# A small second transform on quarters of TensorE, with its neighbours' banks and small passes rearranged

## The chip, the cores and the metric

One core of one Trainium2 chip. The metric is the time of one execution in device microseconds (us). Engines: PE is TensorE (matrix products), DVE VectorE, ACT ScalarE, POOL GpSimd, SP the engine that issues nearly all DMAs here.

## What is computed

The reference runs three layers, one behind the other, in fp32:

```python
# x: (8, 3072, 256)
X = np.fft.rfft(x, axis=1)
Yr = Xr @ w_r - Xi @ w_i + b_r
Yi = Xr @ w_i + Xi @ w_r + b_i
# soft threshold of Yr and Yi at 0.01
y = np.fft.irfft(Yr + 1j * Yi, n=3072, axis=1)      # -> 24576 tokens x 256
logits = y @ phi                                     # 32 slots
d = exp(logits - logits.max(0)); d /= d.sum(0)       # over all tokens
slot_out = experts(d.T @ y)                          # relu(s @ w1[e]) @ w2[e]
c = softmax(logits, axis=1)
z = c @ slot_out
h = z @ w_in;  solu = h * softmax(h);  out = layernorm(solu) * g_ln @ w_out
```

## The kernel before

The program has two phases. Phase 1 (`phase1`, some 600 us) does everything up to the slots' sums; phase 2, which the change leaves alone, does the experts and the last layer over 192 blocks of 128 tokens.

Phase 1 takes the 8 batches b one after the other. A batch's transform over 3072 positions is split: 3072 = 96 x 32. The **first transform** (`stage1`, line 242, or `stage1_first` for batch 0, line 232) works along the 96, in eight units u of a batch; its products, here `s` in the trace (PSUM tile `s1`, two banks), use four quarters of the PE array of 64 rows by 64 columns. ACT copies them to SBUF (`asb`), and SP stores them to a DRAM tensor `ad` (`a_fold`, `a_out`), from which `load_ap` reads `apt` in another order. The **second transform** (`stage2`, line 273) turns `apt` with the constants `d2_sb` into the spectrum `xps` (PSUM, one bank): four products per tile t, each of 128 rows by 128 columns. Half of the entries of `d2_sb` are zero, since the even and the odd frequencies each need 64 of the 128 rows. A batch has 12 such tiles t.

Of `xps` ACT makes a copy of the imaginary part (`xi`, line 291) and the rounded copy `xh` (line 292), DVE the sum `xsum` (line 293) and the rest `xl` (line 294). For t = 0 DVE also makes `xd` and its two parts, and zeros one column of `xh` and `xl` (lines 295 to 303, `zero4`). `stage2s` rounds the sum: `sh` on ACT, `sl` on POOL (line 309). `mix` (line 313) multiplies with the weights into `pb` and `pa`; DVE adds (`yb`, lines 337 and 341) and clips (line 349), POOL subtracts (`s`, line 350). `st_transpose` (line 355) turns `s` on PE into the PSUM tile `sps`, a bank of its own from the pool `pst`, and ACT copies it to `st` (line 369). The bank count of phase 1 is `ps1` 2, `psx` 1, `psy` 2 (`pb`, `pa`), `pst` 1, `psm` 2: eight, all there are.

From `st` a chain of **small products** computes logits, slot softmax and slot sums of the batch: `qt`, `qtr`, `e2`, `inv1`, `ltr`, `maxt`, `maxb`, `fwd1`, `dtr`, `fwd2`, `slots`, `sums`. Each writes a PSUM tile from `pm()`, a ring of two banks (`psm`): a new tile takes the bank of the one before the last, so its first product waits until that one has been read. In the trace they go by what they read: `qt_sb`, `q_sb`, `r_sb`, `lt_sb` (their copies are `lg_sb`), `mx`, `d_sb`, `dt_sb` (copies: `dm_sb`), `dm_sb,w_sb`, and `s,dh_sb` for the slots, whose result DVE adds to `acc` (line 777). A running maximum over the batches (`mrun`, `rescale`, `rexp`) gives two factors `mexp`; with them DVE rescales `acc` (line 756) and `srun` (line 814).

The order of the work is a list: one loop over the 96 tiles calls the large steps, and `tick()` (four times in each round) runs what `after(lag, ...)` has put on a heap for that tick; the lags stand in the table `LAG`. Every engine runs its own instructions strictly in this order. One round, called a step here and named by the t that `mix` takes, is on PE:

```python
s1_next(need); tick(); stage2(t + 1); tick()
st_transpose(t - 2); tick()
stage2s(t + 1); mix(t); tick()
```

that is: a small product or none, `s` (in 8 of 12 steps), `xps` of the next tile, small products, the transposes of `s` of two tiles before, small products, `pb`, `pa`.

Of the kernel before, what the change touches and what calls it, by code (L numbers as in the profile page):

```python
# [35 lines left out]
def kernel(  # L36
# [109 lines left out]
    def phase1(pl: ExitStack, pr_: ExitStack):  # L146
# [84 lines left out]

        def stage1_first(ch):
            if ch == 0:
                ad[0] = dram2.tile([32, 4, 24, D], F32, name="ad", tag="ad")
            dst = s_p.tile([96, 2, D], F32, name="a0", tag="s")
            after(LAG["a_out"], a_out, 0, 2 * ch, 2, dst)
            pool, tag = ((ps1, "s1"), (pst, "sps"), (psm, "pm"))[ch % 3]
# [17 lines left out]
        def a_fold(b, n, t):  # L255
            for c in range(2):
                SP.dma_start(out=ad[b][n:n + 4, 2 * c:2 * c + 2].rearrange("n k g d -> (k g) n d"), in_=t[64 * c:64 * c + 48])

        def a_out(b, n, k, t):
            SP.dma_start(out=ad[b][n:n + k].rearrange("n k g d -> (k g) n d"), in_=t)  # L260
# [366 lines left out]

        def dsub(b, z):
            sl = slice(16 * z, 16 * z + 16)
            lg = small["lg", b].rearrange("p a (l s) -> p (a l) s", l=4)[:, sl]  # L630
            m = small["mb", b].rearrange("p (o s) -> p o s", o=1).to_broadcast([96, 16, 32])
            DVE.tensor_tensor(out=small["d", b][:, sl], in0=lg, in1=m, op=ALU.subtract)
# [947 lines left out]
```

## Time and profile before

| | |
|---|---|
| time, median of 3 runs | 1306.96 us (1306.07 to 1310.65) |
| profiled execution, its own time | 1307.97 us |
| its span, first to last instruction | 1306.2 us |
| phase 1, until the experts' first product | some 598 us |
| PE busy | 1263.1 us (97%) |
| DVE / ACT / POOL busy | 1127.9 / 988.0 / 1010.7 us |
| mean granted clock of TensorE | 0.993 |

The profile is of one execution. Busy time of PE counts products in flight, so a high share alone doesn't tell that PE is at its peak; the chain of work that ended last, the busy time of single stretches, and the instructions in order of time do. Instructions that run into each other on an engine (ACT starts one about 0.1 us before the one ahead of it ends) are each listed with their full length.

### The profile page before, as it was taken

The page shows a single profiled execution, that of the slowest core. Times are in us where ns is not written, and L with a number is a line of the kernel's source. Part 1 is how long each engine was busy: PE and PEld are TensorE (multiplying, and loading weights), DVE is VectorE, ACT ScalarE, POOL GpSimd, SP SyncE. Part 2 cuts the span into 40 slices and gives each one's busy share as a digit, 9 for nine tenths or more (in the row PEclk, how much of TensorE's full clock was granted, in tenths as well). Part 3 has the DMA queues.
Part 4 walks back from the last instruction along what each step waited for, and adds up shares of the span by engine and source line. Part 5 has one row for each costly group of instructions (what it writes and reads, how often), then busy time and mean ns, then how long its engine had stood idle before and what let it go on. Part 6 is the DMA issues. An engine that isn't in the chain of part 4 may idle for free.

```text
span 1306.2 us, 30976 instructions
## 1 busy us (share of the span) xinstructions
PE 1263.1 (97%) x11042; PEld 1115.7 (85%) x11042; DVE 1127.9 (86%) x1568; ACT 988.0 (76%) x1831; POOL 1010.7 (77%) x1114
## 2 busy tenths in 40 slices
PE   6989999999999999899699999999999999999998
PEld 2867878787878878865699999999999999999998
DVE  1867887888788888765999999999999999999995
ACT  3545556565656565543799999999999999999996
POOL 0868686877778775433589999999999999998995
PEclk8999999999999999999999999999999999999999
DMA  8986465564747364259467777777777787777874
GB/s 269 279 229 191 125 176 165 142 198 122 203 118 223 100 200 144 93 186 351 99 168 203 194 192 208 178 196 195 187 203 180 185 229 191 187 198 178 211 180 127
DMA packets 181338, 241.79 MB, mean 185 GB/s; under 512 B 21984, under 2 KB 137056, under 8 KB 181184
## 3 DMA queue, kind: packets, MB, share of 16 engines
q1 hardware_dynamic: 180736, 238.62, 67.2%
q8 instruction: 88, 1.44, 0.5%
q10 hardware_dynamic: 448, 1.18, 0.3%
q14 instruction: 66, 0.54, 0.1%
HBM read 92.00 MB, written 59.11 MB: 116 GB/s over the span
## 4 chain that ended last, share of the span: by engine, by line
PE 82%; DVE 7%; DMA 3%; issue 2%; POOL 2%; ACT 2%; SPq 1%; DVEq 0%; ACTq 0%; POOLq 0%
PE po L89 37%; PE pb L89 9%; PE pm L89 8%; PE xps L89 7%; PE hps L89 6%; PE s L89 5%; PE pa L89 4%; PE sps L92 2%; DVE st L1167 2%; DVE u L1182 2%; PE hps L92 2%; DMA xc<-in_x_dram 1%; PE pm L92 1%; DMA t<-tb 1%; DVE tb L1205 1%
## 5 line engine op out<-in xcount | busy, mean ns | idle before, releaser
L1277 POOL TENSOR_TENSOR ul<-t,uh 128x512 fp32r<-128x512 f32 x336 | 431.2, 1301 | 43.4 <-ACT uh L1263 42.6
L89 PEld LDWEIGHTS po<-gw,uh 128*128 128x128 f32 x2736 | 347.3, 188 | 14.0
L89 PE MATMUL po<-gw,uh 128*128 128x256 f32 x2736 | 353.6, 280 | 0.0
L1167 DVE TENSOR_REDUCE st<-hps 128x1 f32<-128x1024 f32 x192 | 229.1, 1194 | 10.3 <-PE hps L89 10.3
L1182 DVE SCALAR_TENSOR_TENSOR u<-hps,e 128x1024 f32<-128x1024 f32 x192 | 232.1, 1209 | 0.5 <-ACT e L1174 0.3
L1174 ACT ACTIVATE e<-hps,st 128x1024 f32<-128x1024 f32 x192 | 215.4, 1122 | 16.8 <-DVE st L1167 16.8
L89 PE MATMUL po<-gw,ul 128*128 128x256 f32 x1620 | 228.1, 284 | 0.0
L1287 ACT ACTIVATE sq<-u,st 128x1024 f32<-128x1024 f32 x192 | 223.0, 1161 | 0.3 <-DVE u L1182 0.3
L1205 DVE STREAM_TRANSPOSE tb<-u 128x1024 f32<-128x1024 f32 x169 | 210.5, 1246 | 5.9
L89 PEld LDWEIGHTS po<-gw,ul 128*128 128x128 f32 x1620 | 206.1, 188 | 1.1
L350 POOL TENSOR_TENSOR s<-yb,s 128x512 f32<-128x512 f32 x95 | 124.4, 1310 | 103.9 <-DVE s L349 99.9
L1263 ACT ACTIVATE uh<-t 128x768 fp32r<-128x768 f32 x169 | 143.4, 849 | 0.0
L89 PEld LDWEIGHTS xps<-d_sb,apt 128*128 128x128 f32 x768 | 95.0, 194 | 54.7 <-issue 28.5
L89 PE MATMUL xps<-d_sb,apt 128*128 128x128 f32 x768 | 111.3, 288 | 11.8 <-DMA apt<-ad 7.8
L252 ACT ACTIVATE asb<-s 128x1024 f32<-128x1024 f32 x56 | 57.6, 1028 | 79.9 <-PE s L89 71.8
L89 PE MATMUL hps<-gst,ct 128*128 128x512 f32 x338 | 106.2, 396 | 7.5 <-DVE u L1182 6.1
L309 POOL TENSOR_TENSOR sl<-xsum,sh 128x256 fp32r<-128x256 f32 x93 | 78.0, 838 | 34.9 <-ACT sh L308 34.4
L225 POOL TENSOR_TENSOR x<-xc 112x512 f32<-112x512 f32 x56 | 72.1, 1288 | 39.8 <-DMA xc<-in_x_dram 37.0
L293 DVE TENSOR_TENSOR xsum<-xps,xi 128x256 f32<-128x256 f32 x96 | 39.8, 414 | 66.1 <-ACT xh L292 48.9
L1338 ACT ACTIVATE osb<-po,st 128x256 f32<-128x256 f32 x192 | 80.3, 475 | 8.3 <-PE po L89 4.5
L337 DVE TENSOR_TENSOR yb<-pb,bias 128x512 f32<-128x512 f32 x96 | 65.5, 683 | 18.6 <-PE pb L89 18.1
L349 DVE TENSOR_SCALAR s<-yb 128x512 f32<-128x512 f32 x95 | 75.2, 792 | 1.0
(237 smaller groups left out, 2375.6 us busy)
## 6 DMA issues: line engine op xcount, KB each, us to landing
t<-tb SPq DMA_DIRECT2D x676, 128.0 KB, 2.8
xc<-in_x_dram SPq DMA_DIRECT2D x128, 192.0 KB, 3.8
apt<-ad SPq DMA_DIRECT2D x96, 256.0 KB, 4.1
out_dram<-osb SPq DMA_DIRECT2D x47, 512.0 KB, 3.7
ad<-asb SPq DMA_DIRECT2D x112, 192.0 KB, 3.5
ct<-c_dram SPq DMA_DIRECT2D x96, 128.0 KB, 3.9
wt<-in_moe_w_dram SPq DMA_DIRECT2D x21, 512.0 KB, 9.0
ws<-in_moe_w_dram SPq DMA_DIRECT2D x22, 256.0 KB, 6.1
```

The source lines that it names most:

```text
L89: PE.matmul(out=out, lhsT=lhsT, rhs=rhs, start=start, stop=stop)
L309: (POOL if (b, t) > (0, 2) else DVE).tensor_tensor(out=sl, in0=sm_, in1=sh.bitcast(F32), op=ALU.subtract)
L349: DVE.tensor_scalar(out=s, in0=y, scalar1=-LAM, scalar2=LAM, op0=ALU.max, op1=ALU.min)
L350: POOL.tensor_tensor(out=s, in0=y, in1=s, op=ALU.subtract)
L1167: DVE.tensor_reduce(out=st[:, 0, k:k + 1], in_=hps[i], op=ALU.min, axis=AX.X)
L1174: ACT.activation(out=e, in_=hps[i], func=AF.Exp, bias=st[:, 0, k:k + 1], scale=-1.0, accum_out=st[:, 1, k:k + 1])
L1182: DVE.scalar_tensor_tensor(out=u, in0=hps[i] if turned(i) else hps.pop(i), scalar=1.0, in1=et.pop(i), op0=ALU.mult, op1=ALU.mult, accum_ou ...
L1205: DVE.transpose(out=t, in_=ut[i])
L1263: ACT.activation(out=w[:, 0:HA], in_=v[:, 0:HA], func=AF.Copy)
L1277: (DVE if n and i >= NI - 4 else POOL).tensor_tensor(out=ul[:, z, :].rearrange("p c (a j) -> p c a j", a=4), in0=v, in1=w.bitcast(F32), op ...
L1287: ACT.activation(out=sq, in_=ut.pop(i), func=AF.Square, bias=st[:, 2, k:k + 1], scale=-float(DFF), accum_out=st[:, 3, k:k + 1])
L1338: ACT.activation(out=o[:, k], in_=pot.pop(i), func=AF.Copy, scale=stt[j][:, 4, k:k + 1])
```

## The change

1. **Second transform.** Each product of 128 by 128 becomes four of 64 rows by 64 columns, one for each quarter of the PE array (rows k, columns h), so that the zero half of `d2_sb` is left out. The two row halves k go to two PSUM banks: `psx` takes two. `d2_sb` has half its size, and ACT and DVE read `xps` and write `xi`, `xh`, `xsum`, `xl` with patterns that put the columns where they were. `ad` is stored as [2, 32, 2, 24, D], so that one k lies in 64 neighbouring partitions; batch 0 is stored with `a_fold` too, from tiles of `wa_p`.
2. **Banks.** The bank for it comes from `pst`, which is gone: `st_transpose` takes its tile from `pm()`, the ring of two.
3. **Small passes.** `xd` lies in PSUM (the unused part of `xps`). `mb` isn't copied: both subtractions of the maximum read it from PSUM, in `maxb` itself, one behind the other, and the exponentials (`dexp`) come one tick earlier. The four copies of the slot maximum are one reduction. The running maximum is kept negated, one column per batch, so that `rescale` is one reduction, and ACT computes both factors with a bias and rescales `acc` and `srun`.

```diff
-        pst = right("pst", 1, space=PSUM)
...
-            ps = psx.tile([128, 2, 2, 2, 64], F32, name="xps", tag="xps")
+            ps = psx.tile([128, 2, 512], F32, name="xps", tag="xps")
+            v = ps[:, :, 0:256].rearrange("p k (c a g j) -> p k c a g j", c=2, a=2, g=2)
             for gp in range(2):
+                m = d2_sb[:, 8 * q + 2 * tq + gp, :].rearrange("p (c j) -> p c j", c=2)
                 for dh in range(2):
-                    mm(
-                        ps[:, dh, :, gp, :],
-                        a[:, gp, tq % 2, dh * 128:(dh + 1) * 128],
-                        d2_sb[:, 8 * q + 2 * tq + gp, :].rearrange("p (c j) -> p c j", c=2),
-                    )
+                    for z in range(2):
+                        for k in range(2):
+                            h = (k + z) % 2
+                            r = slice(64 * k, 64 * k + 64)
+                            d = 128 * dh + 64 * h
+                            mm(v[64 * h:64 * h + 64, k, :, dh, gp, :], a[r, gp, tq % 2, d:d + 64], m[r])
...
-            ACT.activation(out=xi, in_=psv[:, :, 1, :], func=AF.Copy)
-            ACT.activation(out=hi, in_=psv, func=AF.Copy)
-            DVE.tensor_tensor(out=sm_, in0=psv[:, :, 0, :], in1=xi, op=ALU.add)
-            DVE.tensor_tensor(out=lo, in0=psv, in1=hi.bitcast(F32), op=ALU.subtract)
+            ACT.activation(out=iv, in_=pv[:, :, 4:8], func=AF.Copy)
+            ACT.activation(out=hv, in_=pv, func=AF.Copy)
+            DVE.tensor_tensor(out=sv, in0=pv[:, :, 0:4], in1=iv, op=ALU.add)
+            DVE.tensor_tensor(out=lv, in0=pv, in1=hv.bitcast(F32), op=ALU.subtract)
...
-                xd = xt_p.tile([128, 2, 1], F32, name="xd", tag="xd", bufs=1)
+                xd = ps[:, 0, 256:258].rearrange("p (a o) -> p a o", o=1)
...
-                ps = pst.tile([128, 2, 2, 128], F32, name="sps", tag="sps")
+                ps = pm([128, 2, 2, 128])
...
-            DVE.tensor_reduce(out=m4[:, 0, :], in_=ps.rearrange("o (l s) -> o s l", l=4), op=ALU.max, axis=AX.X)
-            m4_copies(m4)
+            max_slots(m4, ps)
...
-            mb = sm("mb", [96, 32])
-            DVE.tensor_copy(out=mb, in_=ps[0:96, 0:32])
-            small["d", b] = sm("d_sb", [96, 32, 32])
-            small["mb", b] = mb
+            d = small["d", b] = sm("d_sb", [96, 32, 32])
+            m = ps[0:96, 0:32].rearrange("p (o s) -> p o s", o=1).to_broadcast([96, 16, 32])
+            lg = small["lg", b].rearrange("p a (l s) -> p (a l) s", l=4)
             for z in range(2):
-                after(LAG["dsub"] + z, dsub, b, z)
-                after(LAG["dexp"] + z, dexp, b, z)
+                DVE.tensor_tensor(out=d[:, 16 * z:16 * z + 16], in0=lg[:, 16 * z:16 * z + 16], in1=m, op=ALU.subtract)
+                after(LAG["dexp"] - 1 + z, dexp, b, z)
...
-            DVE.tensor_reduce(out=mnew, in_=mrun, op=ALU.max, axis=AX.X)
-            DVE.tensor_scalar(out=mexp, in0=mrun, scalar1=mnew, scalar2=None, op0=ALU.subtract)
-            DVE.tensor_copy(out=mrun[:, 0:1], in_=mnew)
+            DVE.tensor_reduce(out=mrun[:, 2 * b + 2:2 * b + 3], in_=mrun[:, 2 * b:2 * b + 2], op=ALU.min, axis=AX.X)
...
-            ACT.activation(out=mexp, in_=mexp, func=AF.Exp)
+            ACT.activation(out=mexp, in_=mrun[:, 2 * b:2 * b + 2], func=AF.Exp, bias=mrun[:, 2 * b + 2:2 * b + 3], scale=-1.0)
+            ACT.activation(out=acc, in_=acc, func=AF.Copy, scale=mexp[:, 0:1])
+            ACT.activation(out=srun, in_=srun, func=AF.Copy, scale=mexp[:, 0:1])
...
-                DVE.tensor_scalar(out=acc, in0=acc, scalar1=mexp[:, 0:1], scalar2=None, op0=ALU.mult)
...
-                DVE.tensor_scalar(out=srun, in0=srun, scalar1=mexp[:, 0:1], scalar2=None, op0=ALU.mult)
```

What this makes of the order, at three places. PE, the steps t = 7 and t = 8 of a batch, in the changed kernel (`pm<-ident,s` are the transposes of `s`, the two products of `m` and `ones` share one tile):

```order
L89 MATMUL s_4212<-x_3994,fold 64x512 x4
L89 MATMUL xps<-d_sb,apt 64x2x32 x16
L92 MATMUL pm<-ident,s 128x128 x4
L89 MATMUL pm<-m_4164,ones 96x32
L89 MATMUL pm<-ones,m_4164 128x1
L92 MATMUL pm<-ident,qt_sb 128x128 x2
...
L89 MATMUL xps<-d_sb,apt 64x2x32 x16
L89 MATMUL pm<-q_sb,e_sb 128x32
L89 MATMUL pm<-q_sb,e_sb 128x224
L92 MATMUL pm<-ident,s 128x128 x4
L89 MATMUL pm<-f_sb,d_sb 32x96 x16
```

The order of PE's work is what it was; the transposes of `s`, which were `sps<-ident,s` in a bank of their own, now stand in the ring, so the `qt_sb` transposes take the bank of the `s` transposes, and the `d_sb` products that of the `q_sb` products.

ACT, from the copies of `dt_sb` in step t = 9 to the next `st`; first before:

```order
L718 ACTIVATE dt_sb<-pm 128x16x24
L646 ACTIVATE mexp<-mexp 128x2
L291 ACTIVATE xi<-xps 128x256
L292 ACTIVATE xh<-xps 128x512
L728 ACTIVATE dm_sb<-pm 128x512
L369 ACTIVATE st<-sps 128x512
```

and with the change:

```order
L723 ACTIVATE dt_sb<-pm 128x16x24
L649 ACTIVATE mexp<-mrun 128x2
L650 ACTIVATE acc<-acc,mexp 128x256
L651 ACTIVATE srun<-srun,mexp 128x1
L304 ACTIVATE xi<-xps 128x2x4x32
L305 ACTIVATE xh<-xps 128x2x8x32
L733 ACTIVATE dm_sb<-pm 128x512
L382 ACTIVATE st<-pm 128x512
```

Two passes stand between the factors and `xi`.

DVE, the work on `xps` of t = 0 and up to the sum of the slots, with the change:

```order
L311 TENSOR_TENSOR xps<-xi,xps 128x2
L312 COPY xsum<-xps 128x2
L313 CAST xd_h<-xps 128x2
L314 TENSOR_TENSOR xd_l<-xps,xd_h 128x2
L316 CAST xh<-zero_172 128x4
L316 CAST xl<-zero_172 128x4
L350 TENSOR_TENSOR yb<-pb,bias 128x512
L354 TENSOR_TENSOR yb<-yb,pa 128x512
L837 SCALAR_TENSOR_TENSOR dec<-dec,dm 128x512
L362 TENSOR_SCALAR s<-yb 128x512
L688 STREAM_TRANSPOSE ct_sb<-c_sb 96x2x256
L780 SCALAR_TENSOR_TENSOR acc<-pm,mexp,acc 128x256
```

`xd` is read from PSUM, the two casts of zeros stay, the rescaling of `acc` that stood ahead of `yb` is gone, and the sum into `acc` keeps its place.

## Rows read from the trace of the kernel before

**Rows 1.** The page: busy time by engine, and the chain by line.
```profile
PE 1263.1 (97%) x11042; PEld 1115.7 (85%) x11042; DVE 1127.9 (86%) x1568; ACT 988.0 (76%) x1831; POOL 1010.7 (77%) x1114
PE po L89 37%; PE pb L89 9%; PE pm L89 8%; PE xps L89 7%; PE hps L89 6%; PE s L89 5%; PE pa L89 4%; PE sps L92 2%; DVE st L1167 2%; DVE u L1182 2%; PE hps L92 2%; DMA xc<-in_x_dram 1%; PE pm L92 1%; DMA t<-tb 1%; DVE tb L1205 1%
```
**Rows 2.** By stretches: length, busy PE, PEld, DVE, ACT, POOL (instructions), clock, DMA share, GB/s.
```profile
372.94:441.30 68.36, 68.17 (x711) 55.42 (x708) 58.37 (x98) 41.33 (x83) 52.72 (x47) 1.00 0.58 163
...
53.18:57.83 4.65, 4.65 (x41) 3.71 (x40) 3.92 (x7) 2.81 (x6) 4.65 (x5) 1.00 1.00 312
395.99:400.64 4.65, 4.65 (x42) 3.71 (x40) 3.88 (x6) 2.80 (x6) 4.65 (x5) 1.00 0.85 229
```
**Rows 3.** The chain in order of time: start, length, what; two batches.
```profile
211.19 0.89 PE xps L89 x8
...
216.24 0.80 PE pm L89 x32
217.03 1.09 PE xps L89 x8
...
382.74 1.02 PE s L89 x8
383.76 1.09 PE xps L89 x8
```
**Rows 4.** In order of time, one `s` product; then its group by form.
```profile
302.60 0.21 PEld L89 LDWEIGHTS s<-x,fold 48*64 48x64 f32 x8 [0.41 <-issue]
302.60 1.09 PE L89 MATMUL s<-x,fold 48*64 48x512 f32 x8
...
L89 PE MATMUL s<-x,fold 48*64 48x512 f32 x416 | 56.6, 615 | 0.0
```
**Rows 5.** In order of time, step t = 7 of one batch.
```profile
275.18 1.03 ACT L252 ACTIVATE asb<-s 128x1024 f32<-128x1024 f32 x1 [0.64 <-PE s L89]
276.30 0.39 ACT L291 ACTIVATE xi<-xps 128x256 f32<-128x256 f32 x1
276.58 0.59 ACT L292 ACTIVATE xh<-xps 128x512 fp32r<-128x512 f32 x1
277.05 0.44 PE L92 MATMUL pm<-ident,qt_sb 128*128 128x128 f32 x2
277.06 0.61 ACT L369 ACTIVATE st<-sps 128x512 f32<-128x512 f32 x1
```
**Rows 6.** In order of time, steps t = 8 and t = 9 of the same batch.
```profile
279.42 1.05 PE L89 MATMUL xps<-d_sb,apt 128*128 128x128 f32 x8
281.45 0.87 PE L89 MATMUL pm<-f_sb,d_sb 96*32 96x96 f32 x32
283.71 0.63 ACT L448 ACTIVATE r_sb<-pm 128x256 f32<-128x256 f32 x1
285.89 0.20 ACT L646 ACTIVATE mexp<-mexp 128x2 f32<-128x2 f32 x1
287.23 0.60 PE L92 MATMUL pm<-ident,dt_sb 128*128 128x128 f32 x4
```
**Rows 7.** In order of time, step t = 0 of the next batch.
```profile
300.50 1.73 DVE L300 CAST xd_h<-xd 128x2 fp32r<-128x2 f32 x1
301.48 0.72 POOL L309 TENSOR_TENSOR sl<-xsum,sh 128x256 fp32r<-128x256 f32 x1
302.49 0.35 DVE L756 TENSOR_SCALAR acc<-acc,mexp 128x256 f32<-128x256 f32 x1
305.05 0.60 PE L92 MATMUL sps<-ident,s 128*128 128x128 f32 x4
305.80 0.40 DVE L777 SCALAR_TENSOR_TENSOR acc<-pm,mexp,acc 128x256 f32<-128x256 f32 x1
```
**Rows 8.** In order of time, POOL and PE in step t = 5.
```profile
401.12 0.93 POOL L309 TENSOR_TENSOR sl<-xsum,sh 128x256 fp32r<-128x256 f32 x1
402.59 0.39 PE L89 MATMUL pa<-wc_h,sl 128*128 128x256 f32 x2
```

More of the change, by code (lines that the diff above doesn't have):

```diff
@@ L77 @@
     ones = glob.tile([128, 128], F32, name="ones")
-    mrun = glob.tile([128, 2], F32, name="mrun")
+    mrun = glob.tile([128, 2 * B + 2], F32, name="mrun")
     mnew = glob.tile([128, 1], F32, name="mnew")
@@ L169, in phase1 @@
         fold = k_p.tile([128, 128], F32, name="fold")
-        d2_sb = k_p.tile([128, 24, 128], F32, name="d2_sb")
+        d2_sb = k_p.tile([128, 24, 64], F32, name="d2_sb")
         wc_h = k_p.tile([128, 2, 768], F32R, name="wc_h")
@@ L230, in xdiff @@
             after(1, load_x, i + 2)
+        a0 = {}
         def stage1_first(ch):
             if ch == 0:
[L234 to L237, printed above, removed]
+                ad[0] = dram2.tile([2, 32, 2, 24, D], F32, name="ad", tag="ad")
+            if ch % 2 == 0:
+                a0[0] = wa_p.tile([128, 4, D], F32, name="a0", tag=("asb", "x1")[ch // 2 % 2])
+            n = 2 * (ch % 2)
+            dst = a0[0][0:96, n:n + 2]
+            if ch >= 14:
+                after(LAG["a_out"], a_fold, 0, 2 * ch, a0[0][:, n:n + 2], 48)
+            elif n:
+                after(LAG["a_out"], a_fold, 0, 2 * ch - 2, a0[0], 48)
+            pool, tag = ((ps1, "s1"), (psy, "pb"), (psm, "pm"))[ch % 3]
             ps = pool.tile([96, 2, D], F32, name="s1", tag=tag)
@@ L253, in stage1, with a_fold @@
             after(LAG["a_out"], a_fold, b, 4 * u, dst)
[L255 removed]
+        def a_fold(b, n, t, p=64):
             for c in range(2):
[L257 to L260 removed]
+                SP.dma_start(out=ad[b][c, n:n + t.shape[1]].rearrange("n r g d -> (r g) n d"), in_=t[p * c:p * c + 48])
         apt = {}
@@ L359, in st_transpose @@
                 for c in range(2):
-                    ps = psx.tile([128, 2, 128], F32, name="spx", tag="xps") if c else pst.tile([128, 2, 128], F32, name="sps", tag="sps")
+                    ps = psx.tile([128, 2, 128], F32, name="spx", tag="xps") if c else pm([128, 2, 128])
                     for eh in range(2):
@@ L469, in last_chain @@
             m3, nm = sm("m3", [128, 3]), sm("mx2", [128, 2])
-            DVE.tensor_copy(out=m3[:, 0:1], in_=mrun[:, 0:1])
+            DVE.tensor_scalar(out=m3[:, 0:1], in0=mrun[:, 2 * b:2 * b + 1], scalar1=-1.0, scalar2=None, op0=ALU.mult)
             dt = small["dt", b] = sm("dt_sb", [128, 8, 4, 32])
@@ L626, in maxb @@
             after(LAG["csoft"], csoft, b)
[L628 to L632, printed above, removed]
         def dexp(b, z):
@@ L1516, in _consts @@
     D2[0, :, 0:2, :, 0] = Dm[1, 0:2, :, :, 0].transpose(1, 0, 2, 3)
-    d2 = D2.transpose(1, 2, 0, 3, 4, 5).reshape(128, 3, 2, 4, 128).transpose(0, 1, 3, 2, 4).reshape(128, 24, 128)
+    d2 = np.zeros((2, 32, 2, 24, 2, 32))
+    for k1p in range(2):
+        d2[k1p] = D2[:, :, 2 * k1p:2 * k1p + 2, :, k1p].transpose(1, 2, 0, 3, 4)
+    d2 = d2.reshape(128, 3, 2, 4, 64).transpose(0, 1, 3, 2, 4).reshape(128, 24, 64)
     e2 = Dw.transpose(3, 4, 5, 0, 1, 2).reshape(128, 2, 128)
```

35 lines of the change are left out of this document (19 added, 16 removed).

## The prediction

> **What bounds the kernel now.** I read the page first: TensorE (PE) is busy 97% of the span, and in the chain that ended last nearly every large entry is PE's; `xps`, the second transform that the change rewrites, is 7% of the span [rows 1]. The reader is to see that a cheaper `xps` can pay only while PE stays the engine that is waited for. The busy time by stretches says how far that holds in phase 1. One batch (68.36 us, 12 steps) has PE busy 68.17 us, so PE never waits; DVE has 58.37 and POOL 52.72 [rows 2]. But in single steps with an `s` product POOL is busy 4.65 of 4.65 us, and in the one of the first batch the DMA engines are full as well [rows 2]. There POOL is level with PE.
>
> Third, the chain in order of time gives prices by position. `s` costs 1.02 us and `xps` behind it 1.09; `xps` behind `pa` costs 0.89; 32 quarter-column products cost 0.80; `xps` behind those costs 1.09 [rows 3]. So `xps` pays 0.20 when it follows products that run in part arrays. The granted clock is 1.00 in these stretches, the 2.4 GHz level [rows 2].
>
> **Part 1: `xps` in four quarters.** An fp32 product is two instructions: eight `xps` of 128 columns take 0.89, so 0.111 each, which is 128 columns twice at 2.4 GHz. The 32 small products have 96 columns and run four side by side: 8 rounds of 0.080 are 0.64, leaving 0.16 for filling and draining. `s` is 2 rounds of 0.427, leaving 0.17. The new `xps` is 32 instructions of 64 columns in 8 rounds of four: 8 x 0.053 = 0.43, plus 0.17, plus the 0.20 that now falls on the full-array product behind it: 0.80. Behind `s`, in the same shape, filling is paid once: 0.85 + 0.43 + 0.17 + 0.20 = 1.65 against 1.02 + 1.09 = 2.11. I take gains of 0.43 behind `s` (a little for the loads), 0.28 behind column products (1.09 - 0.80) and 0.08 behind `pa` (0.89 - 0.80). By the order a batch has six, four and two of these: 2.58 + 1.12 + 0.16 = 3.9 us. Seven batches give 27, the last, without `s`, about 2: **29 us if PE alone decided**.
> The far end of this price: eight 64-column weight loads of `s` take 0.21 us, 0.026 each; were 32 of them to come one after the other, 0.84 instead of 0.43. But the eight products, 4.9 us at 615 ns each, are through in 1.09 [rows 4]: quarters work side by side. I take the near end.
>
> **Part 2: transposes of s in the ring of two `pm` banks.** Each `pm` tile now waits until the tile two before it has been read out. Nothing is added to PE, but PE is in order, so everything behind waits too. I go through the batch by the tile t that `pb` mixes.
> - t=7. The order gives `s` transposes, two tiny products in one tile, then the `qt_sb` transposes, which now wait for ACT's `st`. ACT is held by `asb` from 275.18 for 0.92 (the next can start 0.1 before an end), then `xi` (0.28) and `xh` (0.48) [rows 5]: `st` starts at 276.86 however fast `xps` is, and ends at 277.46. `qt_sb` starts at 277.50 instead of 277.05: **+0.45**, and the gain of 0.43 is gone.
> - t=8. `d_sb` products wait for `r_sb`. Before, it came at 283.71 [rows 6], behind an exponential of `d_sb` on ACT; the change runs that one a tick earlier. Then it follows `xh`, and ends about 0.85 (the new `xps` until ACT sees it) + 0.28 + 0.48 + 0.63 = 2.25 us after `xps` starts; now the products start 2.0 after it (281.45 against 279.42). **+0.25.**
> - t=9. The second `dt_sb` transposes wait for `dm_sb`. Here the change also puts the rescaling of acc and srun on ACT ahead of `xi`: about 0.3 (256 columns, as `xi`) and 0.15 behind the 0.2 of `mexp` (285.89) [rows 6]. `xi` 286.55, `dm_sb` 287.31 to 287.91, transposes 287.97 instead of 287.23: **+0.75**.
> - t=6: the `s` transposes wait for the copy of the first `lt_sb` products, and the `mx` product behind them waits for such a copy before as now: taken as 0. t=10: -0.08. t=11: the second `w_sb` waits for `st`, -0.15 is left.
> - t=0. The transposes wait for DVE's acc sum, 305.80 to 306.20, while they start at 305.05 [rows 7]. DVE loses its acc scaling (0.35) [rows 7] but stays in order: about 305.9, **+0.85**.
>
> **Part 3: DVE's small passes.** The cast of two elements at t=0 lasts 1.73 us and ends when POOL's `sl` ends at 302.20 [rows 7]: a DVE pass from SBUF to SBUF that stands still while POOL works. The change reads it from PSUM. Two casts of the same kind, the zeros into `xh` and `xl`, stay 0.3 us behind it, and POOL is busy until the same 302.20, so I let them inherit the wait and count 0.35 for DVE, not 1.5. The Trainium skill, "SBUF — State Buffer" (Who interferes with whom), says that casts and `tensor_scalar` between SBUF operands can take a port pair that GpSimd shares, and that the second to come is blocked whole. By that rule the zeros wait and the sum stands; without it the third rival below holds. The row agrees. The other removed copies, the reductions and the two subtractions now in one place lie beside PE's work: nothing. What covers them is DVE's idle time, 10 of 68.36 us in a batch [rows 2]; where it is gone, `yb` at t=7 comes later by one subtraction, which then stands ahead of it.
>
> **Part 4: POOL in the steps with `s`.** At t=1 to 5 PE would win 0.28 + 4 x 0.43 = 2.0, less the 0.85 of t=0: 1.15. But in the step at t=5 POOL's `sl` ends at 402.05 and the `pa` that needs it starts at 402.59 [rows 8]: 0.54 of room, behind a step in which POOL never idled [rows 2]. Beyond that PE waits for `sl`. I take **-0.6** for t=0 to 5, between 0 and -1.15.
>
> **Start and DMA.** The a0 tiles, the new layout of `ad` and the halved d2 move the same bytes, or less, in runs of the same length; two more DMA issues stand at the end of the first stage, against two `xps` ahead of the first `pb` that get shorter. Nothing, within 2 us, about the length of those two `xps`. The first batch is full on POOL and DMA [rows 2], so it gains nothing; the last has the waits of t=0 and 95 against about 2 us: nothing. Phase 2 isn't touched.
>
> **Sum.** Per batch -0.6 + 0 + 0.45 + 0.25 + 0.75 - 0.08 - 0.15 = +0.6; six batches 3.7 us. The profiled execution took 1307.97 (span 1306.2), 1.0 above the median of 1306.96: 1311.7 against the one and **1310 us**, rounded down, against the other. What the quarters give, the shared ring and POOL take back.
>
> **Rivals.**
> 1. The gain stays: every read-out on ACT starts with the end of `xps`, so it moves forward too, and POOL may have more room than one `sl` shows. Half of the 29 us: 1293; all: 1278. For it: PE busy 68.17 of 68.36. Against: t=7, where ACT is held by `asb`.
> 2. Slower, POOL: if the steps with `s` gain nothing, the 0.85 of t=0 stays in view and the waits of t=7 to 9 add their 1.45: 2.1 a batch, 13 us for six, 2 for the last: 1322. It decides where `sl` has less than about 0.2 us of room at t=5. For it: 4.65 of 4.65. Against: POOL gets the time back in the waits at t=0.
> 3. The zero casts don't wait (the change does what it says): DVE is 1.5 us earlier at t=0, so t=0 wins its 0.43 and POOL's later work moves up with it: -2.4 for t=0 to 5, +1.2 behind, -1.2 a batch, 1300. Against: the same kind of pass at the same place.
> 4. Slower, the quarters don't overlap their loads: 0.84 for 0.43. `xps` is then 1.21 behind column products instead of 1.09, 0.05 better behind `s`, 0.32 worse behind `pa`, and every read-out on ACT that a ring wait hangs on comes 0.4 later: about +4 a batch, 1335. The Trainium skill, "TensorE: Matmul & The Clock Gate" (Wait — 56ns, not 53.3ns?), has a floor of about 25 ns between the starts of matmuls however small they are; that would make 32 of them 0.80. Against it: eight products through in 1.09 that last 4.9 together [rows 4]; and 32 products of 96 columns within 0.80, which a floor of 25 ns would just fill, so that row can't decide.
>
> **Numbers.** Forecast 0.45, rivals 0.20, 0.20, 0.08, 0.07. The forecast's own range, with start, last batch and t=0 to 5 between their bounds, is 1303 to 1317. To hold 8 in 10 I reach into rivals 1 and 2: **1294 to 1323**. About 0.5% (6.5 us) is what a measurement of this kernel can tell from no change. Faster by more than that, under 1300.4: most of rival 1, part of 3 and a little of the forecast, 0.23. Slower, over 1313.5: most of 2, all of 4 and the forecast's upper end, 0.31. Within: 0.46.
>
> **What would show it.** In the profile after: `xps` behind `s` at about 0.6 in the chain and not 1.09; PE waiting for ACT `st`, `r_sb`, `dm_sb` and DVE acc before `pm` products, some 0.5 to 1 us each, six or seven times; the 1.7 us of the cast on the zero casts; PE waiting for POOL `sl` near t=5. PE's busy time should fall by some 25 us while the span doesn't. I am wrong if those waits are missing, or if `xps` still takes about 1 us.

## The result and the profile after

The changed kernel takes **1322.62 us** (median of 4 runs, 1320.98 to 1328.64) against 1307.47 of the kernel before on the same chip: ratio **1.0125**, 95% interval 1.0104 to 1.0145. It is slower by 15 us, where 1310 was forecast. The profiled execution took 1328.64, 6.0 above the median; so single batches are compared below, not ends.

The page of the changed kernel: span, busy time, the chain by line.
```profile
span 1326.8 us, 35529 instructions
...
PE 1252.9 (94%) x13346; PEld 1095.7 (83%) x13346; DVE 1123.2 (85%) x1529; ACT 990.3 (75%) x1843; POOL 1008.3 (76%) x1114
...
PE po L89 37%; PE pb L89 7%; PE pm L89 6%; PE hps L89 6%; PE pa L89 3%; PE pm L92 3%; PE s L89 3%; PE xps L89 3%; DMA xc<-in_x_dram 2%; DVE st L1169 2%; DVE u L1184 2%; PE hps L92 1%; ACT xh L305 1%; POOL x L228 1%; POOL x L224 1%
```
Against [rows 1], `xps` fell from 7% of the chain to 3% and PE's busy time by 10 us, and yet the span grew: PE's share fell from 97% to 94%, and POOL's `x` and ACT's `xh` are on the chain, where PE stood nearly alone.

From here on **step t** runs from the start of `pb(t)` to that of `pb(t+1)`; the work that the prediction tells under t stands ahead of `pb(t)`, so at the end of step t-1. A batch and two of its steps (columns as in [rows 2]):
```profile
384.11:454.26 70.15, 65.88 (x999) 52.08 (x997) 57.26 (x92) 41.43 (x86) 51.99 (x48) 1.00 0.57 159
403.87:408.62 4.75, 4.49 (x66) 3.56 (x64) 4.02 (x5) 2.70 (x6) 4.75 (x6) 1.00 0.50 112
408.62:417.85 9.23, 7.67 (x139) 5.97 (x137) 9.06 (x12) 5.73 (x12) 8.86 (x9) 1.00 1.01 305
```
PE's work in a batch fell from 68.17 to 65.88 us, while the batch grew from 68.36 to 70.15: 4.27 us of waiting where there were 0.19. This table gives the steps of the sixth batch, from the starts of the first `pb` product in each trace; the names of the runs are those of the experiments below.

| kernel | t=0 to 5 | sum | t=6 to 11 | sum |
|---|---|---|---|---|
| before | 5.67 4.64 5.87 5.08 4.65 7.77 | 33.68 | 6.51 5.00 5.34 3.43 6.57 7.81 | 34.68 |
| changed | 5.41 4.22 5.44 4.69 4.75 9.23 | 33.74 | 7.01 5.38 6.38 3.36 6.61 7.67 | 36.41 |
| e1 own bank with pa | 5.40 4.22 5.61 4.69 5.22 8.13 | 33.27 | 6.06 5.46 5.06 3.73 7.83 7.43 | 35.57 |
| e2 c_lo on DVE | 5.41 4.22 5.44 4.69 4.22 8.18 | 32.17 | 7.01 5.38 6.38 3.36 6.61 7.67 | 36.41 |
| e3 both | 5.40 4.22 5.62 4.70 4.82 7.41 | 32.16 | 6.07 5.46 5.06 3.73 7.96 7.43 | 35.70 |
| e4 before + ring | 5.67 4.64 5.87 5.08 4.65 8.32 | 34.23 | 7.16 6.24 6.18 3.44 7.00 8.00 | 38.00 |
| e5 pa mixed | 5.40 4.22 5.62 4.69 4.83 7.43 | 32.19 | 6.06 5.46 5.05 3.36 6.61 7.43 | 33.97 |
| e6 e3, no quarters | 5.72 4.69 5.91 5.12 4.69 7.84 | 33.97 | 6.53 5.19 5.35 3.73 7.81 7.86 | 36.47 |
| e8 acc, srun on DVE | 5.41 4.22 5.44 4.69 4.83 9.57 | 34.16 | 7.00 5.36 5.79 3.36 6.61 8.12 | 36.25 |
| e9 no quarters | 5.72 4.69 5.91 5.12 4.69 8.40 | 34.53 | 7.21 5.61 6.39 3.49 7.05 7.86 | 37.60 |

(In three other batches of the changed kernel t=11 is 7.93 to 7.95, and t=6 to 11 sum to 36.7.)

**Steps t=0 to 5: the quarters pay, and POOL takes it back.** PE in order of time, changed kernel:
```profile
406.72 1.09 PE L89 MATMUL s<-x,fold 48*64 48x512 f32 x8
407.63 0.65 PE L89 MATMUL xps<-d_sb,apt 64*64 64x64 f32 x32
408.20 0.66 PE L92 MATMUL pm<-ident,s 128*128 128x128 f32 x4
...
410.37 0.40 PE L89 MATMUL pa<-wc_l,sh 128*128 128x256 f32 x2
411.58 0.50 PE L89 MATMUL pa<-wc_h,sl 128*128 128x256 f32 x2 [0.81 <-POOL sl L322]
412.21 0.97 PE L89 MATMUL pm<-ft_sb,r_sb 128*32 128x96 f32 x32
...
417.35 0.63 PE L92 MATMUL pm<-ident,s 128*128 128x128 f32 x4 [0.61 <-ACT lg_sb L605]
```
`s` and `xps` take 1.48 us from start to start where they took 2.11 [rows 3], and steps t=0 to 3 are shorter by 0.26, 0.42, 0.43 and 0.39. Then `pa` waits for POOL's `sl`. The `sl` passes of the two kernels, before first:
```profile
383.78 1.23 POOL L309 TENSOR_TENSOR sl<-xsum,sh 128x256 fp32r<-128x256 f32 x1
...
389.77 1.22 POOL L309 TENSOR_TENSOR sl<-xsum,sh 128x256 fp32r<-128x256 f32 x1
...
395.78 0.97 POOL L309 TENSOR_TENSOR sl<-xsum,sh 128x256 fp32r<-128x256 f32 x1
```
```profile
393.19 1.26 POOL L322 TENSOR_TENSOR sl<-xsum,sh 128x256 fp32r<-128x256 f32 x1
...
399.22 1.25 POOL L322 TENSOR_TENSOR sl<-xsum,sh 128x256 fp32r<-128x256 f32 x1
...
405.24 0.99 POOL L322 TENSOR_TENSOR sl<-xsum,sh 128x256 fp32r<-128x256 f32 x1
...
410.63 0.90 POOL L322 TENSOR_TENSOR sl<-xsum,sh 128x256 fp32r<-128x256 f32 x1
```
Counted from `pb(0)` (374.73 and 384.11) they start at 9.05, 15.04, 21.05 and, with [rows 8], 26.39 before; at 9.08, 15.11, 21.13 and 26.52 after. POOL keeps its own time, and PE, 1.5 us earlier by t=3, arrives early and waits. The chain of waits (start, length, what) stays on POOL through the steps before t=5, and then goes through DVE to `r_sb`, for which the next small products wait:
```profile
402.08 0.73 POOL ct_sb L708
402.81 1.23 POOL x L224
404.05 1.26 POOL x L228
405.30 0.94 POOL sl L322
...
408.71 1.00 DVE s L362
...
410.87 1.30 DVE r_sb L473 x2
...
412.21 0.97 PE pm L89 x24
```
DVE is late there because its clip `s` stands still beside POOL's passes. It lasts 2.23 us in the changed kernel, as it did before (2.22), 0.99 in e5, where POOL has less to do, and 0.42 at t=11 of the changed kernel, where POOL is idle. First the changed kernel, then `r_sb` and its products in the kernel before, then e5:
```profile
408.71 2.23 DVE L362 TENSOR_SCALAR s<-yb 128x512 f32<-128x512 f32 x1
```
```profile
399.24 2.22 DVE L349 TENSOR_SCALAR s<-yb 128x512 f32<-128x512 f32 x1
401.38 1.29 DVE L460 STREAM_TRANSPOSE r_sb<-r_sb 128x512 f32<-128x512 f32 x2
402.91 0.96 PE L89 MATMUL pm<-ft_sb,r_sb 128*32 128x96 f32 x32
```
```profile
387.65 0.99 DVE L362 TENSOR_SCALAR s<-yb 128x512 f32<-128x512 f32 x1
```
**Steps t=6 to 11: the ring.** PE, same kernel and batch: three products that wait for the tile two before them in the ring to be read out, and what ACT does ahead of the last of them.
```profile
424.66 0.44 PE L92 MATMUL pm<-ident,qt_sb 128*128 128x128 f32 x2 [0.87 <-ACT st L382]
...
429.43 0.87 PE L89 MATMUL pm<-f_sb,d_sb 96*32 96x96 f32 x32 [0.32 <-ACT r_sb L461]
...
436.20 0.66 PE L92 MATMUL pm<-ident,dt_sb 128*128 128x128 f32 x4 [1.11 <-ACT dm_sb L733]
```
```profile
433.89 0.29 ACT L649 ACTIVATE mexp<-mrun 128x2 f32<-128x2 f32 x1
434.21 0.51 ACT L650 ACTIVATE acc<-acc,mexp 128x256 f32<-128x256 f32 x1
434.63 0.28 ACT L651 ACTIVATE srun<-srun,mexp 128x1 f32<-128x1 f32 x1
434.81 0.36 ACT L304 ACTIVATE xi<-xps 128x256 f32<-128x256 f32 x1
```
Steps t=6, 7 and 8 are longer by 0.50, 0.38 and 1.04.

### The profile page after: what moved, and what is told of

Read it like the earlier page. It is cut to its first block, busy times and chain, and to the rows that moved or that the text cites. A ratio compares the mean times of both kernels' runs of the same rounds, so it can differ in the third digit from the quotient of the medians.

```text
span 1326.8 us, 35529 instructions
## 1 busy us (share of the span) xinstructions
PE 1252.9 (94%) x13346; PEld 1095.7 (83%) x13346; DVE 1123.2 (85%) x1529; ACT 990.3 (75%) x1843; POOL 1008.3 (76%) x1114
## 4 chain that ended last, share of the span: by engine, by line
PE 70%; DVE 10%; ACT 6%; POOL 5%; issue 5%; DMA 4%; SPq 1%; DVEq 0%; ACTq 0%; POOLq 0%
PE po L89 37%; PE pb L89 7%; PE pm L89 6%; PE hps L89 6%; PE pa L89 3%; PE pm L92 3%; PE s L89 3%; PE xps L89 3%; DMA xc<-in_x_dram 2%; DVE st L1169 2%; DVE u L1184 2%; PE hps L92 1%; ACT xh L305 1%; POOL x L228 1%; POOL x L224 1%
## 5 line engine op out<-in xcount | busy, mean ns | idle before, releaser
L89 PEld LDWEIGHTS xps<-d_sb,apt 64*64 64x64 f32 x3072 | 60.7, 139 | 46.9 <-issue 23.1
L89 PE MATMUL xps<-d_sb,apt 64*64 64x64 f32 x3072 | 67.4, 226 | 12.0 <-DMA apt<-ad 8.1
```

The costliest lines, as they stand in the source:

```text
L89: PE.matmul(out=out, lhsT=lhsT, rhs=rhs, start=start, stop=stop)
```

## The experiments

The theory: POOL sets t=0 to 5, so that nothing of the quarters' gain is left there, and waits in the shared ring of two `pm` banks stretch t=5 to 8; the two are separate. The rivals: the waits come from the passes moved to ACT and not from the ring; `sl` is late because DVE and ACT deliver late; the quarters are worth nothing. All times are medians; ratios are to the kernel before on the same chip, where it takes 1306.8 to 1307.7, so times are compared as they are.

| run | us | ratio, 95% interval |
|---|---|---|
| e1 transposes of s in pa's bank | 1310.15 | 1.0024 (1.0014 to 1.0034) |
| e2 c_lo on DVE | 1311.75 | 1.0031 (1.0020 to 1.0042) |
| e3 both | 1302.63 | 0.9968 (0.9956 to 0.9981) |
| e4 before + ring | 1334.91 | 1.0204 (1.0185 to 1.0223) |
| e5 e3, s(8) and s(9) in the ring | **1295.66** | 0.9911 (0.9895 to 0.9927) |
| e6 e3 with full-array xps | 1318.09 | 1.0086 (1.0070 to 1.0102) |
| e7 before, c_lo on DVE | 1305.19 | 0.9983 (0.9972 to 0.9994) |
| e8 changed, acc and srun on DVE | 1323.42 | 1.0119 (1.0101 to 1.0138) |
| e9 changed, full-array xps | 1333.54 | 1.0198 (1.0184 to 1.0211) |
| e10 before + small passes | 1306.66 | 0.9994 (0.9985 to 1.0003) |
| e11 e5, 32 bytes put back | **1294.74** | 0.9910 (0.9893 to 0.9928) |
| e12 e5, other banks | 1296.90 | 0.9926 (0.9914 to 0.9939) |

**e1.** No bank is free all the time, but pa's stands empty for a part of each step: `pa` is to be read out before the next transposes of s, and they before the next `pa`.
```diff
-                ps = pm([128, 2, 2, 128])
+                ps = psy.tile([128, 2, 2, 128], F32, name="sps", tag="pa")
```


> The changed kernel with one edit: the transposes of s leave the ring of the two pm banks and take turns with pa in pa's bank. Ring theory: the +2.0 us that steps t=6 to t=11 of a steady batch gained (34.68 to 36.67) are waits for a pm bank to be read out (qt_sb, d_sb, dt_sb behind st, r_sb, dm_sb), so they go and the gain of the quarters shows there: t=6 to 11 at 33.0 to 34.7, total 12 to 22 us below the changed kernel, 1300 to 1310. Steps t=0 to 5 stay at 33.7, since POOL sets them. Rival: the waits come from the passes that were moved to ACT (acc, srun), and the bank has no part: t=6 to 11 stays above 36, total within 3 us of 1322. Third: transposes that now wait for DVE's second sum out of pa give part back: t=9 and 10 longer by up to 0.6 each.


1310.15, 12.5 below the changed kernel. The waits in t=6 and t=8 are gone (6.06, 5.06), and the 0.61 behind `lg_sb`: t=4 and t=5 together lose 0.63 (13.98 to 13.35). The third expectation came in as well, and larger: t=9 and t=10 grew by 0.37 and 1.22, behind DVE's sums, and t=7 is 5.46, since the transposes wait 0.29 for DVE's `yb` there. So the ring made the waits; t=6 to 11, at 35.57, missed the expected 33.0 to 34.7 by what the new waits cost.

**e2.**
```diff
-            POOL.tensor_tensor(out=f[:, z_], in0=f[:, z_].bitcast(F32), in1=ch[:, z_].bitcast(F32), op=ALU.subtract)
+            DVE.tensor_tensor(out=f[:, z_], in0=f[:, z_].bitcast(F32), in1=ch[:, z_].bitcast(F32), op=ALU.subtract)
```


> The changed kernel with one edit: the four quarter passes that make the low part of c (0.73 us each, on POOL in steps t=1 to 4) run on DVE. POOL theory: steps t=0 to 5 last 33.7 us in both kernels because POOL's work sets them, and 2.9 us less of it lets t=4 and t=5 lose their waits for sl: t=0 to 5 at 31.3 to 32.0, total 11 to 16 us below the changed kernel, 1306 to 1312. Rival: the waits for sl come from DVE and ACT, which deliver xsum and sh late, and POOL is only the last in the row: no change, within 3 us of 1322. Third: DVE has no room for 1.6 us more in these steps, slower by 2 to 8.


1311.75, 10.9 below. t=4 and t=5 fall by 0.53 and 1.05, every other step of the batch stays to 0.01 us. In the third batch t=5, 13.29 in the changed kernel, is 8.30: the long waits there were POOL's too. POOL's load is the cause, not what is handed to it.

**e3.** Both edits.


> The changed kernel with both edits. If ring and POOL are separate costs in separate steps, the gains add: 1322 less 12 to 22 less 11 to 16, about 1288 to 1298, below the kernel before. If one of them only hides behind the other, the sum is no better than the better one alone, about 1302 to 1308.


1302.63: 20 us below the changed kernel, where e1 and e2 sum to 23. They add, nearly; the level missed its range, since e1's own loss at t=9 and t=10 stayed. By its time alone it lies where "no better than the better one" was expected; the steps decide, since t=0 to 5 are e2's (32.16) and t=6 to 11 e1's (35.70). Its trace shows the wait behind that loss, on PE and on DVE:
```profile
431.37 0.63 PE L92 MATMUL sps<-ident,s 128*128 128x128 f32 x4 [1.61 <-DVE yb L354]
```
```profile
427.71 2.17 DVE L743 STREAM_TRANSPOSE dm_sb<-dm_sb 128x512 f32<-128x512 f32 x2
429.80 0.64 DVE L350 TENSOR_TENSOR yb<-pb,bias 128x512 f32<-128x512 f32 x1
430.53 0.69 DVE L354 TENSOR_TENSOR yb<-yb,pa 128x512 f32<-128x512 f32 x1
```
**e4.** The ring alone, on the kernel before.
```diff
-        pst = right("pst", 1, space=PSUM)
...
-            pool, tag = ((ps1, "s1"), (pst, "sps"), (psm, "pm"))[ch % 3]
+            pool, tag = ((ps1, "s1"), (psy, "pb"), (psm, "pm"))[ch % 3]
...
-                ps = pst.tile([128, 2, 2, 128], F32, name="sps", tag="sps")
+                ps = pm([128, 2, 2, 128])
```


> The kernel before with the shared ring alone: full-array second transform, small passes on DVE, but the transposes of s in the two pm banks. Ring theory: the waits show without anything else of the change; t=8 is then the dearest, since the r_sb copy comes behind the exponential of d_sb on ACT as before (283.71 against 281.45, +2.3), t=7 +0.45, t=9 +0.6, t=0 +0.7 to 1.2: 3 to 4.5 a batch, 1327 to 1338. If the waits need the moved ACT passes, it stays within 5 us of 1307.


1334.91, +27 us; t=5 to 8, t=10 and t=11 are longer, by 3.9 us a batch in all. Every wait is there without the moved passes (PE, one batch):
```profile
421.74 0.63 PE L92 MATMUL pm<-ident,s 128*128 128x128 f32 x4 [0.72 <-ACT lg_sb L592]
429.20 0.44 PE L92 MATMUL pm<-ident,qt_sb 128*128 128x128 f32 x2 [0.60 <-ACT st L368]
434.83 0.87 PE L89 MATMUL pm<-f_sb,d_sb 96*32 96x96 f32 x32 [1.16 <-ACT r_sb L447]
441.39 0.66 PE L92 MATMUL pm<-ident,dt_sb 128*128 128x128 f32 x4 [0.64 <-ACT dm_sb L727]
451.19 0.93 PE L89 MATMUL pm<-dm_sb,w_sb 128*64 128x32 f32 x8 [0.22 <-ACT st L368]
```
**e5.**
```diff
-                ps = psy.tile([128, 2, 2, 128], F32, name="sps", tag="pa")
+                ps = pm([128, 2, 2, 128]) if t in (8, 9) else psy.tile([128, 2, 2, 128], F32, name="sps", tag="pa")
```


> The kernel of the third run with one edit: the transposes of s(8) and s(9), which waited 0.34 and 1.6 us for DVE's second sum out of pa's bank, go back to the pm ring; the ten others stay in pa's bank. If that wait is all that stretched t=9 and t=10 (3.73 and 7.8 us against 3.36 and 6.61 with the ring), both go back to the ring's lengths: 1.5 a batch, 10 us in all, 1291 to 1296. Rival: the wait moves on to the second w_sb product behind them in the ring (t=10 or 11 longer by 0.5): 1295 to 1299. Third: DVE's sums are late for pb and pa anyway, no change, 1300 to 1304.


1295.66: t=9 and t=10 are 3.36 and 6.61. It beats both kernels, by 12 and by 27 us. Its sixth batch:
```profile
363.39:429.55 66.16, 65.32 (x998) 52.05 (x997) 55.12 (x97) 41.45 (x87) 49.42 (x44) 1.00 0.59 169
```
PE waits 0.84 us of it, against 4.27 in the changed kernel.

**e6.** `stage2`, `load_ap`, the first stage and d2 as before, the rest as in e3.
```diff
-            ps = psx.tile([128, 2, 512], F32, name="xps", tag="xps")
+            px = psx.tile([128, 2, 2, 2, 2, 64], F32, name="xps", tag="xps")
+            ps = px[:, 0]
...
-                    for z in range(2):
-                        for k in range(2):
-                            h = (k + z) % 2
-                            r = slice(64 * k, 64 * k + 64)
-                            d = 128 * dh + 64 * h
-                            mm(v[64 * h:64 * h + 64, k, :, dh, gp, :], a[r, gp, tq % 2, d:d + 64], m[r])
+                    mm(
+                        ps[:, dh, :, gp, :],
+                        a[:, gp, tq % 2, dh * 128:(dh + 1) * 128],
+                        d2_sb[:, 8 * q + 2 * tq + gp, :].rearrange("p (c j) -> p c j", c=2),
+                    )
```


> The kernel of the third run with the second transform on the full array again (128 columns, old layout of ad and of d2); shared use of pa's bank, the passes moved off DVE and POOL's relief all stay. It prices the quarters alone where ring and POOL no longer take the gain back. By the steps (t=0 to 5 longer by 1.5 to 1.9, t=6 to 11 by about 1.2, since the waits for pa's bank at t=9 and 10 take some): 3 a batch, 1318 to 1326. If the quarters were worth the whole 3.9: 1330. Rival: they are worth nothing even so, and what the third run won on the kernel before came from the other edits: 1300 to 1308.


1318.09: where POOL has room, the quarters are worth 15.5 us, 2.57 a batch. PE's busy time in the batch is 4.02 apart (65.17 in e3, 69.19 here); the rest goes into waits, 2.70 in e3 and 1.25 here.

**e7.** e2's edit on the kernel before.


> The kernel before with the four passes for the low part of c on DVE. POOL theory: POOL was level with PE in t=0 to 5 but did not set their length (0.54 us of room at t=5), so relief brings little: 1303 to 1308, and steps t=0 to 4 stay at 5.67, 4.65, 5.87, 5.08, 4.65. Rival: those passes cost the kernel before as much as the changed one, and the gain of the second run has nothing to do with the quarters: 1294 to 1299.


1305.19: 2.5 us, and t=0 to 4 are 5.68, 4.64, 5.87, 5.08 and 4.65. What it won lies in single stalls, as at t=5 of the third batch (7.77 for 9.20). POOL was level there and not over; it is the quarters that made its load a cost.

**e8.**
```diff
-            ACT.activation(out=acc, in_=acc, func=AF.Copy, scale=mexp[:, 0:1])
-            ACT.activation(out=srun, in_=srun, func=AF.Copy, scale=mexp[:, 0:1])
...
+                DVE.tensor_scalar(out=acc, in0=acc, scalar1=mexp[:, 0:1], scalar2=None, op0=ALU.mult)
...
+                DVE.tensor_scalar(out=srun, in0=srun, scalar1=mexp[:, 0:1], scalar2=None, op0=ALU.mult)
```


> The changed kernel with the scaling of acc and srun back on DVE at their old places. The step t=8 took 1.05 us more than before; if ACT's two passes ahead of xi make 0.45 of that, as the prediction counted, it falls by 0.3 to 0.6 a batch: 1318 to 1321, t=8 at 5.8 to 6.1. If they make none of it, 1321 to 1324; if nearly all, 1314 to 1316 (t=8 at 5.4).


t=8 is 5.79, so the two passes made 0.59 of its 1.04; but the time is 1323.42, no gain, where 1318 to 1321 was expected: t=11 is 8.12 (7.67 before the edit). At its end the transposes of s wait 0.51 for DVE's acc sum and POOL's `s`, which end at 448.28 and 448.33 in that trace. Counted from `pb(11)`, DVE begins the sums ahead of them 0.46 later than in the changed kernel: 0.26 is the scaling itself, back at its place ahead of `yb`, and 0.20 is PE's earlier coming. So a part of what the edit won is its own price on DVE, and a part was room that ended at the next wait. In the three batches ahead of it t=11 grew by 0.44, 0.23 and 0.44; the 0.34 at t=5 here (9.23 to 9.57) is not seen there.

**e9.** e6's edit on the changed kernel, ring and POOL as there.


> The changed kernel with the second transform on the full array again: ring and moved passes stay. It prices the quarters inside the change as made. From the ring alone (1334.9) the earlier exponential of d_sb should take some 0.9 a batch back and acc and srun on ACT cost 0.5: 1329 to 1334, so that the quarters are worth 7 to 11 us in the changed kernel, all of it in t=6 to 11 and nothing in t=0 to 5 (33.7 to 34.2 in both). If the quarters were worth nothing beside the ring and POOL: 1320 to 1325.


1333.54: the quarters are worth 10.9 us in the change as made. By the table they win 0.8 in t=0 to 5 and 1.2 in t=6 to 11. "Nothing in t=0 to 5" was wrong by that 0.8: it took the stretch without quarters for as long as in the kernel before, and it is 0.85 longer, mostly by the ring's wait for `lg_sb` (0.72, t=5 8.40).

**e10.** The small passes alone, on the kernel before, with `xd` in SBUF as there; for example
```diff
-            DVE.tensor_reduce(out=m4[:, 0, :], in_=ps.rearrange("o (l s) -> o s l", l=4), op=ALU.max, axis=AX.X)
-            m4_copies(m4)
+            max_slots(m4, ps)
...
-                after(LAG["dsub"] + z, dsub, b, z)
-                after(LAG["dexp"] + z, dexp, b, z)
+                DVE.tensor_tensor(out=d[:, 16 * z:16 * z + 16], in0=lg[:, 16 * z:16 * z + 16], in1=m, op=ALU.subtract)
+                after(LAG["dexp"] - 1 + z, dexp, b, z)
```


> The kernel before with the small passes of DVE removed or given to ACT, and nothing else: full-array second transform, own bank for the transposes of s. The prediction gave these passes nothing but what the ring makes of them, since PE is busy without a break: 1304 to 1310, t=8 at 5.34 or up to 0.2 more. If DVE's load was a cost of its own in the kernel before: 1298 to 1303. If ACT's two more passes make PE wait even without the ring: 1311 to 1314, t=8 at 5.8.


1306.66: nothing, as the prediction had it, and t=8 stays 5.34.

**e11 and e12.** The traces showed something that no theory had: `pb` and `pa` products start 120 ns apart in the changed kernel and 117 before; it is 120 in e1 to e3, e5, e6, e8 and e9, which all lack the tile `xd` in SBUF (e6 and e9 have no quarters), and 117 in e4, e7 and e10, which have it. The removed `xd` (32 bytes) had shifted `xh`, `xl`, `sh` and `sl` in SBUF, and the banks had moved too. One edit for each:
```diff
+                xt_p.tile([128, 8], F32, name="pad", tag="pad", bufs=1)
```


> The kernel of the fifth run with one tile of 32 bytes put back at the place in SBUF where xd was, so that xh, xl, sh and sl begin at multiples of 64 bytes again, as in the kernel before (in the changed kernel they begin 32 bytes behind one). The products pb and pa start 120 ns apart in the changed kernel and 117 before, over 18 products in 95 steps some 4 us. If the place of xh to sl in SBUF sets that: 116 to 117 ns here and 1290 to 1293. If it doesn't: 120 ns and within 2 us of 1295.7.


```diff
-        psx = right("psx", 1, space=PSUM)
         psy = right("psy", 1, space=PSUM)
+        psx = right("psx", 1, space=PSUM)
```


> The kernel of the fifth run with the banks of pb and pa at 4 and 5 in place of 2 and 3, and xps below them; SBUF as there. If the banks in PSUM set the pace of pb and pa: 116 to 118 ns and 1290 to 1293. If the place in SBUF does: 120 ns and within 2 us of 1295.7.


Twelve products of t=1 lie between the starts of these two rows, in e5, e11 and e12:
```profile
369.35 0.64 PE L89 MATMUL pb<-wc_l,xh 128*128 128x256 f32 x4
370.79 0.40 PE L89 MATMUL pa<-wc_h,sl 128*128 128x256 f32 x2
```
```profile
370.65 0.63 PE L89 MATMUL pb<-wc_l,xh 128*128 128x256 f32 x4
372.06 0.39 PE L89 MATMUL pa<-wc_h,sl 128*128 128x256 f32 x2
```
```profile
368.51 0.64 PE L89 MATMUL pb<-wc_l,xh 128*128 128x256 f32 x4
369.94 0.40 PE L89 MATMUL pa<-wc_h,sl 128*128 128x256 f32 x2
```
With the place in SBUF restored the products start 117.5 ns apart and steps are shorter by 0.04 us (t=1 4.17); with other banks they stay at 119 to 120. So it is the place in SBUF. The total, 1294.74, missed the expected 1290 to 1293 and is inside e5's interval: about 3 us by the steps, which the totals don't resolve.

## Why the prediction was wrong

The forecast was 1310, no change; it is 1322.62, just inside the range and slower by more than 0.5%. It is what the second rival gave (1322), and on its ground, POOL; that its 2.1 a batch is the measured figure is in part luck, since the 0.85 of t=0 in it was not seen and waits that it priced lower fill the place.

- **Part 1, the price of the quarters: right.** 0.43 was forecast behind `s`; steps t=1 to 3 won 0.42, 0.43, 0.39. e3 against e6 shows PE's busy time per batch 65.17 against 69.19: 4.02, where 3.9 was forecast. The fourth rival (loads in series) is out: 32 products start within 0.57 us, 18 ns apart. The Trainium skill, "TensorE: Matmul & The Clock Gate" (Wait — 56ns, not 53.3ns?), has a floor of some 25 ns between starts; on four quarters the trace has 18 and doesn't show it.
- **Part 4, POOL "-0.6 for t=0 to 5": the step that failed.** The room of 0.54 at t=5 was read rightly, but taken for all the room there is, and for a gain that PE keeps. From `pb(0)` to the products of `pa(5)` that take `sl` PE won 0.39 (27.86 to 27.47), and 0.31 of that goes at once: the next products start 0.63 behind them instead of 0.32. Some 0.2 of it is a wait for DVE's `r_sb`, which ends at 412.16; in the kernel before it ended at 402.67 and its products started at 402.91, so the room there was 0.24 and not 0.54. The other 0.1 is the pair itself, whose second product starts 0.22 behind the first instead of 0.11. With +0.13 at the end of t=11 (t=0's own wait) the stretch is at +0.05, where -0.6 was forecast: about the bound 0 that the text named and set aside for the cap. e2 prices POOL's waits there at 1.58 a batch.
- **Part 2, t=6 "taken as 0": +0.15.** The transposes of s wait 0.61 for `lg_sb` there; before, only `mx` behind them waited, for 0.19. The gains of the quarters hide most of it. e4 shows the wait bare: t=5 is 0.55 longer.
- **t=7, t=8: right**, 0.50 against 0.45 and 0.38 against 0.25. e4 shows why t=8 is so small: without the earlier exponential it is 1.24.
- **t=9, 0.75: right mechanism, too small by 0.3.** `mexp`, `acc` and `srun` hold `xi` back by 0.92 (433.89 to 434.81), where 0.65 was counted from `xi`'s 0.3 and a guess. By e8 the two passes make 0.59 of the 1.04, where 0.45 was counted, and the ring the other 0.45, where 0.3 was.
- **t=10 -0.07 (-0.08); t=11 +0.04 (-0.15).** **t=0, +0.85: too large.** Its wait is seen in step 11, +0.13 in most batches. Counted from `pb(11)`, DVE's acc sum ended 1.0 earlier (8.16 to 7.14 in the sixth batch), where 0.3 was counted: POOL's `sl`, behind which the casts end, came 0.4 sooner, the work between it and `yb` is 0.35 shorter, and the scaling that went to ACT is 0.27.
- **Part 3, the zero casts: nearly.** They last 0.58 and 0.78 us, 0.16 each before, and end some 0.03 behind POOL's `c_sb` and `sl`: 1.0 of waiting beside POOL, where the cast of two elements lasted 1.73 [rows 7] and now takes 0.15. The Trainium skill, "SBUF — State Buffer" (Who interferes with whom), blocks the second to come on the shared port; the rows agree. The third rival (no wait) is out, and in e10 the passes changed nothing.
- **"Last batch 0": too low.** From the first `pb` to the last, the last batch grew from 60.07 to 64.36 in the profiled execution, in which the clock fell there twice. In traces without such a fall it takes 61.39 and 61.94 with the ring (e4, e9) and 58.0 to 60.3 with another bank (before, e1, e3, e5, e7, e11): the ring again, 1.3 on the kernel before (e4). The first batch varies between 61 and 68 from trace to trace, so its 0.97 tells nothing.

Summed by the prediction's steps: 0.05 + 0.15 + 0.50 + 0.38 + 1.04 - 0.07 + 0.04 = +2.1 a batch, where +0.6 was forecast; two batches without other stalls show +1.8 and +2.0. Of the 1.5 that lie between, 0.65 are POOL's stretch and 0.3 is t=9. Six batches make 12 of the 15 us and the last at least 1.3. How the rest divides between the first batch and the falls of the clock is not settled, since these differ from one execution to the next.

One forecast for the trace failed: PE's busy time fell by 10 us and not by 25, 2.3 a batch. The missing 1.6 is found in three places, by the busy time of a batch in pairs of runs: the place of the tiles in SBUF (below) takes 0.43 (e5 65.32, e11 64.89), the ring 0.74 (e4 68.91, before 68.17), and the stops for POOL 0.53 (changed 65.88, e2 65.35), 1.7 together. Products beside a wait count as busy for longer: the two of `sl` 0.50 us in the changed kernel and 0.39 before.

## What to carry to other kernels

When PE is made faster in a stretch in which another engine is level with it, don't count the gain there until that engine's own work is shorter, and look for every product that hangs on it, also through a third engine: here `sl` had 0.54 of room, but `r_sb`, through DVE, 0.24. The subtractions for c's low part, 2.9 us of POOL's work, moved to DVE, opened the way. An edit that takes a buffer from its neighbours should be priced alone: the shared ring cost 27 us on the kernel before, against 11 to 16 that the quarters paid, and a bank that stands empty at that time (pa's, for ten of the twelve tiles) did the same service for little.

## What the runs showed of the hardware

**Clock.** Where a wait for POOL was long, TensorE's granted clock fell behind it. Third batch of the changed kernel, three stretches, and PE there:
```profile
191.40:196.00 4.60, 4.04 (x61) 3.17 (x60) 4.50 (x5) 2.70 (x5) 4.60 (x5) 1.00 1.02 281
196.00:200.00 4.00, 2.04 (x38) 1.56 (x40) 3.91 (x7) 0.43 (x1) 3.64 (x4) 0.72 0.97 294
200.00:205.00 5.00, 5.00 (x78) 2.99 (x78) 2.23 (x3) 2.44 (x5) 5.00 (x5) 0.54 0.72 215
```
```profile
196.96 0.50 PE L89 MATMUL pa<-wc_h,sl 128*128 128x256 f32 x2 [1.52 <-POOL sl L322]
198.46 1.55 PE L89 MATMUL pm<-ft_sb,r_sb 128*32 128x96 f32 x32 [1.00 <-DVE r_sb L473]
```
After idle times of 1.52 and 1.00 us the mean clock of the stretches is 0.72 and 0.54, so for most of the second it is at the 1.2 GHz level, and 32 column products take 1.55 instead of 0.97. That step lasted 13.29 us against 9.20 in the kernel before, which also waits 1.00 for `r_sb` at that place, but not for POOL, and keeps a clock of 1.00; in e2, with POOL relieved, it is 8.30. So these waits cost more than their length.

**Place in SBUF.** With the tiles that TensorE reads as weights moved by 32 bytes in SBUF, its products start 120 ns apart and not 117 (e5 against e11; e12, with other banks, stays at 119 to 120). Only this one shift was tried, so whether multiples of 64 bytes are what counts is not shown.
